# A planned attention and MLP kernel: the first theta tiles keyed four steps sooner, one threshold operation for two heads, and new cost numbers in the planner

## The chip, the core and the metric

The kernel runs on one core of one Trainium2 chip. The time is device microseconds of one launch, the median of several runs. The engines are named as in the profile: PE is the matmul engine and PEld its weight loads, DVE the vector engine, ACT the scalar engine, POOL the GpSimd engine, SP the queue that issues the transfers.

## The reference, cut to what matters

Three layers follow each other. B is 4, heads 8, sequence 576, head width 64, model width 512.

```
scores = q @ k.T / 8                         # for each batch and head
thresh = max(scores) - tau                   # row by row
scores = where(scores >= thresh, scores, -1e9)
attn   = exp(scores - max) / (sum + 1e-9);   x = attn @ v

xn = layernorm(x) * g_ln;   x = x + relu(xn @ w_ch1) @ w_ch2      # 512 -> 2048 -> 512

theta = x @ w_theta
y = w_tok_r @ (x * cos(theta)) + w_tok_i @ (x * sin(theta))
u = x + y;   out = u + relu(u @ w_ch)
```

## The kernel before

Nothing is ordered by hand. Each piece of work is an `op` with the engines that could do it and an assumed duration in nanoseconds on each, with its dependencies, with the buffer slots that it takes and frees, and with a key or an offset. `Plan.run` simulates the engines with these assumed durations: at each step it takes the engine and op that could start first, lets an op with several engines go to the one that would end it first (with a penalty for each), and emits it. PE takes the ready op with the lowest key, the other engines the one with the smallest ready time plus `OFF[kind]`. What is emitted is the fixed instruction order of each engine on the chip. So an assumed duration changes no instruction by itself. It changes which engine does an op, and in which order. The lines that the prediction speaks of are these:

- Attention goes over (batch, query tile of 128, head pair): `couple`. Each couple has two heads (`unit`), in the tail tile of 64 rows one. QK fills a PSUM tile S for each head (L720). DVE copies it negated into E and takes the minimum along the row (`top`, L784, tile `bt`). The threshold is `bt + tau` (`thresh`, L791 on ACT, L793 on POOL or DVE, tile `thr`). ACT then does the mask (L797) and the exponential (L800). P, the 16-bit high and low parts of E, is made by L222, L224 or L226 (high) and L229 (low, 512 and 64 columns apart). A transposing transfer turns P, and PE multiplies by v (L748). There are four E slots and two S slots.
- Batch 0's attention comes first. Beside it DVE, ACT and POOL split the first MLP weights into high and low parts by bit operations (`cvt`: L373 to L414, tiles `raw_w`, `a_w`, `w`).
- The MLP goes over six groups of 384 rows, first with the first half of the hidden units (`p_A`, `chA`) between attention couples, then with the second half (`p_B`, L515, and `c`, L538). The order of the second half is `(1,2), (1,0), (1,1), (0,0), (0,1), (0,2)`. A group has eight steps, and each step is one `p_B` of 12 matmuls and the `c` of 9 matmuls of the step before.
- Between them, where PE is assumed idle for more than 200 ns, `keep` puts filler matmuls (L345, tile `warm`).
- The third layer goes over batches: `transposes` (pt, L1241, tile x1T), `thetas` (th, L1288, then t and r on ACT and DVE, L1295 to L1313), `make_z` (sin, cos, products and their high and low parts z, L1363 to L1374 and L229), `mix` (y, L1451, then u, L1473 and L1478, and x1T again from u) and `chan` (o, L1508). In `mix(0)` there are four column blocks of 54 matmuls, and a block takes two of four PSUM slots, which the adds L1473 free. Transposes and thetas of batch 0 have a key in the last MLP group:

```
T0STEP = 5
KEY0 = 2e7 + 5 * nB + T0STEP + 0.3     # nB = 8 steps in a group
```

- The weights of the third layer (`th`, `tok`, `cw`) are split by `cvt` too. The third pair of `tok` tiles, `cw`, and the z tiles take slots that the last MLP group frees, one for each step.

Of the kernel before, what the change touches and what calls it, by code (L numbers as in the profile page):

```python
# [22 lines left out]
KB = 4  # L23
# [173 lines left out]
def tile_kernel(  # L197
# [48 lines left out]
    def gc(n):  # L246
        return 145.0 + 2.11 * n
# [45 lines left out]
    taup = const.tile([128, 1], F32, name="taup")  # L293
# [56 lines left out]
    def cvt(src, shape, hi, lo, name, start=(), acq=(), scales=(), kind="cvt"):  # L350
# [196 lines left out]
    class Keys:  # L547


        def __init__(self, b, hp, prev):  # L550
# [21 lines left out]
            o = op(hi, [o], A=ac(576), V=vc(576, .52), kind=kd)  # L572
# [84 lines left out]
    class Queries:  # L657


        def __init__(self, b, t, prev):  # L660
# [27 lines left out]
            o = op(hi, [o, k_tau], A=ac(512) + 93.0, V=vc(512, .52), kind=kd)  # L688
            self.ready = [op(lo, [o], (), (sraw,), V=vc(512, 1.4), G=2000, kind=kd)]

    def couple(b, t, hp):
# [36 lines left out]
        for w in us:  # L728
            pts.append(unit(w, o_qk, d, whole, pen0, kw, cp, spv, sx_ if w is us[0] else ()))
# [45 lines left out]
    def unit(st, o_qk, d, whole, pen0, kw, cp, spv, sx_):  # L775
# [40 lines left out]
        stp = Slot(rM)  # L816

        def turn_p(e):

            if "o" not in cp:  # L820
                cp["o"] = m_tile(spv, [128, 512], "pv_" + nm)
            st["tp"] = m_tile(stp, [128, 4, 128], "tp_" + nm)
            for t in range(4):
                T.transpose(st["tp"][:, t, :], st["e"][:, t * 128:(t + 1) * 128], ident)
            T.transpose(cp["o"][0:64, 256 + 128 * j:384 + 128 * j], st["e"][:, 512:576], ident)

        def take(e):
            st["pt"] = ap.tile([128, 1280], F16, tag=str(spt), name="PT_" + nm).bitcast(F32).rearrange(
                "p (t q) -> p t q", t=5)
            copy(e, st["pt"][:, 0:4, :], st["tp"])  # L830

        def take_tail(e):
            copy(e, st["pt"][0:64, 4, :], cp["o"][0:64, 256 + 128 * j:384 + 128 * j])
# [5 lines left out]
        if whole:  # L839
            o = op(turn_p, [o_mask, k_pool] + turned[-1:], (stp,) + ((spv,) + sx_ if j == 0 else ()), (es,), T=640,  # L840
                   kind="att", **kw)
            turned.append(o)
            o = op(take, [o], (spt,), (stp,), A=ac(512), V=690, kind="hi16", **kw)
            return op(take_tail, [o], A=265, V=290, kind="hi16", **kw)
        o = op(hi16, [o_mask], (s16,), A=ac(576), V=vc(576, .52), G=gc1(576), kind="hi16", pen=dict(pen0 or {}, A=HPA), **kw)
# [5 lines left out]
    def scaled(tile_):  # L851
# [25 lines left out]
        x_ops[tile_] = [op(scale, [o], V=vc(512), G=gc(512), kind="guard", pen={"G": G0} if p == 0 and t < 4 else None)]  # L877
# [7 lines left out]
    def ln_group(p, gi, base):  # L885
# [42 lines left out]
        for t in range(nt):  # L928
# [37 lines left out]
            o = first = op(norm, [o_rs, first] + last_tr, (sn,), A=808, V=vc(512, .52), kind="ln")  # L966
# [5 lines left out]
            o = op(hi, [o] + xt[:1], () if xt else (sx,), A=ac(512), V=vc(512, .52), G=gc1(512), kind="lnev")  # L972
# [153 lines left out]
    for gidx, (p, gi) in enumerate(order):  # L1126
# [4 lines left out]
        else:  # L1131
# [18 lines left out]
            o = op(hi, [o], A=ac(KB * n), V=vc(KB * n, .52), G=gc1(KB * n))  # L1150
            deps = [op(lo, [o], V=vc(KB * n), G=gc(KB * n))]
# [16 lines left out]
    def split_weight(name, src_list, start):  # L1168
# [22 lines left out]
    for i in range(3):  # L1191
# [5 lines left out]
                                 [load_of(o[-1]) for o in tok_ops])  # L1197
# [429 lines left out]
```

## Time and profile before

| | |
|---|---|
| time, median of 3 runs | 943.57 us (943.29 to 943.91) |
| the profiled execution | 943.46 us, span of its trace 941.6 us |
| mean granted TensorE clock | 0.978 of 2.4 GHz |
| busy share of the span: PE, DVE, ACT, POOL | 94%, 72%, 56%, 57% |
| stages, us from the start of the span | batch 0's attention to 132.7; attention and first MLP half to 451; last group of the first half to 486; second half to 709; third layer to the end |

The span is what the trace covers, and the execution's own time is 1.9 us longer. A row of the timeline gives start, duration, and in brackets how long the engine was idle before and who ended that. PE's durations include the waiting of a pipelined matmul and its ends are modelled, so the starts of two rows tell more than a duration.

### The profile page before, as it was taken

How to read it: one execution, taken by the hardware profiler on the slowest of the kernel's cores; microseconds unless marked ns; L12 is line 12 of the kernel's file. 1: busy time of each engine (PE TensorE's matmuls, PEld its weight loads, DVE VectorE, ACT ScalarE, POOL GpSimd, SP SyncE). 2: the span in 40 equal slices, each digit the busy share in tenths (PEclk: the TensorE clock that was granted, in tenths of full speed). 3: DMA queues.
4: the chain of work that ended last, by engine and by line, in shares of the span. 5: the costliest groups of instructions: out<-in, count | busy, mean ns of one | idle time of the engine just before them, and what ended most of it. 6: DMA issues, size and time to landing. Idle time of an engine off the chain costs nothing. (4 is left out here: it accounts for less than half of the span.)

```text
span 941.6 us, 18946 instructions
## 1 busy us (share of the span) xinstructions
PE 888.4 (94%) x7287; PEld 789.3 (84%) x7287; DVE 677.7 (72%) x1227; ACT 530.2 (56%) x968; POOL 537.7 (57%) x614
## 2 busy tenths in 40 slices
PE   9787879999999999999999999999989899999998
PEld 7665668878888888888888899989977789899998
DVE  6899989788897887783788692221489873697734
ACT  7787778888887878883556561111356330453300
POOL 5999899779887887781556771000266530263400
PEclk9898899999999999999999999999999899999999
DMA  7889796799789988792555660340021111010011
GB/s 195 171 189 184 168 199 119 138 227 176 148 180 174 184 183 145 158 165 48 190 168 168 202 190 7 100 154 1 1 77 57 28 42 39 12 63 1 14 38 51
DMA packets 224954, 111.93 MB, mean 119 GB/s; under 512 B 174048, under 2 KB 206304, under 8 KB 224864
## 3 DMA queue, kind: packets, MB, share of 16 engines
q1 hardware_dynamic: 224576, 110.72, 51.6%
q8 instruction: 57, 0.93, 0.4%
q14 instruction: 33, 0.27, 0.1%
q10 hardware_dynamic: 288, 0.00, 0.0%
HBM read 52.50 MB, written 15.73 MB: 72 GB/s over the span
## 5 line engine op out<-in xcount | busy, mean ns | idle before, releaser
L229 POOL TENSOR_TENSOR P<-E,P 128x64 f16<-128x64 f32 (+1 forms) x194 | 144.4, 759 | 14.6 <-DVE P L224 5.8
L784 DVE TENSOR_SCALAR_CACHE_REDUCE E<-S 128x576 f32<-128x576 f32 x144 | 105.4, 747 | 25.6 <-PE S L720 16.3
L797 ACT ACTIVATE E<-E,thr 128x576 f32<-128x576 f32 x144 | 108.0, 768 | 11.5 <-POOL thr L793 10.1
L515 PE MATMUL p_A<-xt,w 128*128 128x384 f32 x576 | 112.9, 343 | 1.7 <-issue 1.5
L1451 PE MATMUL y<-tok,z 128*128 128x288 f32 x768 | 109.7, 301 | 4.9 <-DVE u L1473 3.7
L515 PE MATMUL p_B<-xt,w 128*128 128x384 f32 x576 | 111.1, 341 | 1.4 <-DVE w L414 1.4
L538 PE MATMUL c<-w,h_B 128*128 128x512 f32 x432 | 108.9, 395 | 3.6 <-DVE h_B L524 2.0
L538 PE MATMUL chA<-w,h_A 128*128 128x512 f32 x432 | 111.0, 400 | 1.4 <-DVE h_A L524 1.4
L1451 PEld LDWEIGHTS y<-tok,z 128*128 128x128 f32 x768 | 106.2, 193 | 5.9 <-DVE u L1473 4.2
L515 PEld LDWEIGHTS p_B<-xt,w 128*128 128x128 f32 x576 | 103.8, 190 | 6.3 <-DVE w L414 2.3
L800 ACT ACTIVATE E<-E,ntaup 128x576 f32<-128x576 f32 x144 | 107.5, 767 | 0.9
L720 PE MATMUL S<-khi,q 64*128 64x288 f32 (+1 forms) x576 | 85.9, 328 | 21.3 <-DVE E L784 18.3
L515 PEld LDWEIGHTS p_A<-xt,w 128*128 128x128 f32 x576 | 98.2, 188 | 5.6 <-issue 4.3
L538 PEld LDWEIGHTS c<-w,h_B 128*128 128x128 f32 x432 | 80.1, 188 | 19.5 <-DVE h_B L524 3.1
L538 PEld LDWEIGHTS chA<-w,h_A 128*128 128x128 f32 x432 | 78.0, 188 | 18.2 <-issue 2.1
L748 PEld LDWEIGHTS <-PT 128*128 128x128 f16 (+1 forms) x2240 | 75.9, 101 | 17.0 <-issue 14.5
L720 PEld LDWEIGHTS S<-khi,q 64*128 64x128 f32 (+1 forms) x576 | 56.8, 192 | 37.6 <-DVE E L784 23.1
L748 PE MATMUL pv<-va,PT 128*128 128x65 f16 (+1 forms) x2240 | 84.1, 195 | 3.4 <-DVE va L224 2.3
L521 ACT ACTIVATE h_B<-p_B 128x384 fp32r<-128x384 f32 x48 | 23.6, 491 | 110.8 <-PE p_B L515 110.8
L524 DVE SCALAR_TENSOR_TENSOR h_B<-p_B,h_B 128x384 fp32r<-128x384 f32 x48 | 26.6, 553 | 72.6 <-ACT h_B L521 72.3
L229 DVE TENSOR_TENSOR P<-E,P 128x512 f16<-128x512 f32 (+1 forms) x94 | 69.6, 759 | 4.9 <-POOL P L226 3.3
L226 POOL TENSOR_SCALAR P<-E 128x576 f16<-128x576 f32 x85 | 64.7, 764 | 14.3 <-ACT E L800 13.0
(194 smaller groups left out, 1704.4 us busy)
## 6 DMA issues: line engine op xcount, KB each, us to landing
raw_w<-in_w SPq DMA_DIRECT2D x32, 512.0 KB, 4.4
raw_tok<-in_wtok SPq DMA_DIRECT2D x12, 432.0 KB, 4.3
qraw<-in_qT SPq DMA_DIRECT2D x20, 256.0 KB, 3.7
vraw<-in_v SPq DMA_DIRECT2D x16, 320.0 KB, 3.8
kraw<-in_kT SPq DMA_DIRECT2D x16, 288.0 KB, 3.2
xscr<-x SPq DMA_DIRECT2D x18, 256.0 KB, 3.1
xl<-xscr SPq DMA_DIRECT2D x18, 256.0 KB, 4.1
out<-uo SPq DMA_DIRECT2D x16, 288.0 KB, 2.1
```

Source lines behind the costliest of these rows:

```text
L226: G.tensor_scalar(out=out, in0=in_, scalar1=1.0, scalar2=0.0, op0=ALU.mult, op1=ALU.add)
L229: e.tensor_tensor(out=out, in0=a, in1=b, op=ALU.subtract)
L515: T.matmul(st["ps"][:, :n], lhsT=ch.w1(a, c), rhs=xt()[:, c, bb, :n], start=(kk == 0), stop=(kk == 11))
L521: A.activation(out=st["h"][:, 0, :n], in_=st["ps"][:, :n], func=AF.Relu)
L524: V.scalar_tensor_tensor(out=st["h"][:, 1, :n], in0=st["ps"][:, :n], scalar=0.0, in1=f(st["h"][:, 0, :n]), op0=ALU.max, op1=ALU.subtract)
L538: T.matmul(ps, lhsT=h[:, a, t * 128:(t + 1) * 128], rhs=ch.w2(bb), start=(first and (a, bb) == M2[0]), stop=(stop and (a, bb) == M2[2]))
L720: T.matmul(w["S"][:, n, 0:288], lhsT=qd.q["t"][r, a, hp], rhs=d.k[bb][r, n * 288:(n + 1) * 288], start=(k == 0), stop=(k == 2))
L748: T.matmul(out[:, j * 65:j * 65 + n], lhsT=l, rhs=r[:, j * 65:j * 65 + n], start=(k == 0), stop=(k == len(seq) - 1))
L784: V.tensor_scalar(out=st["e"].rearrange("p (a k) -> p a k", a=2), in0=st["S"][:, :, 0:288], scalar1=-1.0, scalar2=None, op0=ALU.mult, op1= ...
L797: A.activation(out=st["e"], in_=st["e"], func=AF.Prelu, bias=st["thr"], scale=-1.0, alpha=STEEP)
L800: A.activation(out=st["e"], in_=st["e"], func=AF.Exp, bias=ntaup, scale=1.0)
L1451: T.matmul(st["ps"][n][:, 0:288], lhsT=a, rhs=w[:, n * 288:(n + 1) * 288], start=(k == 0 and q == 0), stop=(k == 8 and q == 2))
```

## The change

Four things are changed. `T0STEP` is 1 and not 5. The minima of two heads stand in one tile `bt` of two columns, and one `thresh` operation adds tau to both, so that it depends on both `top` operations, and both masks depend on it. The splitting of `cw` gets a kind of its own with the offset 25000. Many assumed durations of the planner are raised: DVE's cheap copies from 157 + 0.52 n to 157 + 0.95 n, POOL's two-input operations from 145 + 2.11 n to 145 + 2.5 n, and DVE's two-input operations from 157 + 1.04 n to 157 + 1.5 n in the last phases and in `cvt`. A branch for a mode that is never used (`WHOLE` is empty) is removed. What each operation computes is the same.

```diff
-T0STEP = 5
+T0STEP = 1
+LATE = 25000.0
+GC = 2.5
+V2 = 1.5
-OFF = {..., "cvt": 6000.0}
+OFF = {..., "cvt": 6000.0, "late": LATE}
...
-        return 145.0 + 2.11 * n
+        return 145.0 + GC * n
...
+        for k in range(2):
+            V.tensor_scalar(out=taup2[:, k:k + 1], in0=taub, scalar1=0.0, scalar2=TAU_MAX, op0=ALU.max, op1=ALU.min)
...
-        o = op(s2a, [oa], G=gc1(n), V=vc(n, .52), **kw)
-        o = op(s2b, [o], V=vc(n, .52), **kw)
-        o = op(s2c, [o], (), [sa], V=vc(n), **kw)
+        o = op(s2a, [oa], G=1550.0, V=vc(n, 1.1), **kw)
+        o = op(s2b, [o], V=vc(n, .95), **kw)
+        o = op(s2c, [o], (), [sa], V=vc(n, 1.45), **kw)
...
         def thresh(e):
-            st["thr"] = ap.tile([128, 1], F32, tag="thr", bufs=8, name="thr_" + nm)
-            if e is A:
-                A.activation(out=st["thr"], in_=st["bt"], func=AF.Identity, bias=taup, scale=1.0)
+            m = len(us)
+            cp["thr"] = ap.tile([128, 2], F32, tag="thr", bufs=6, name="thr_" + nm)
+            if e is G:
+                G.tensor_tensor(out=cp["thr"][:, 0:m], in0=cp["bt"][:, 0:m], in1=taup2[:, 0:m], op=ALU.add)
+            elif e is A:
+                A.activation(out=cp["thr"][:, 0:m], in_=cp["bt"][:, 0:m], func=AF.Identity, bias=taup2[:, 0:1], scale=1.0)
...
-        o_top = op(top, [o_qk], (es,), (ss,), V=880, kind="top", **kw)
-        o = op(thresh, [o_top, k_tau], A=280, G=300, V=140, kind="thr", pen=pen0, **kw)
+        st["top"] = op(top, [o_qk], (es,), (ss,), V=830, kind="top", **kw)
+        cp.setdefault("tops", []).append(st["top"])
+        if len(cp["tops"]) < len(us):
+            return None
+        o_thr = op(thresh, cp["tops"] + [k_tau], A=290, G=320, V=160, kind="thr", pen=pen0, **kw)
+        return [u["rest"](o_thr) for u in us]
...
-        o = op(hi16, [o_mask], (s16,), A=ac(576), V=vc(576, .52), G=gc1(576), kind="hi16", pen=dict(pen0 or {}, A=HPA), **kw)
+        o = op(hi16, [o_mask], (s16,), A=ac(576), V=vc(576, .95), G=gc1(576), kind="hi16", pen=dict(pen0 or {}, A=HPA), **kw)
...
-                                 [load_of(o[-1]) for o in tok_ops])
+                                 [load_of(o[-1]) for o in tok_ops], "late")
```

Three places show what this does to the order. In the names, numbers count buffers, so p_B_2_0 is step 0 and c_2_0 the first row tile of the last group, and x12 is the count of equal rows. The lines after the change are up to eight lower.

On PE, in the last MLP group, this stands around the first transposes of batch 0 before the change:

```order
L515 MATMUL p_B_2_4_9822<-xt_0_2_9489,w_8444 128x384 x12
L1241 MATMUL pt_0_0_9841<-ident,xl_0_9408 128x128 x4
L1241 MATMUL pt_0_1_9848<-ident,xl_1_9414 128x128 x4
L1241 MATMUL pt_0_2_9858<-ident,xl_2_9419 128x128 x4
L538 MATMUL c_2_0_9755<-w_8345,h_B_2_3_9813 128x512 x3
L1241 MATMUL pt_0_3_9872<-ident,xl_3_9626 128x128 x4
L538 MATMUL c_2_1_9761<-w_8345,h_B_2_3_9813 128x512 x3
L538 MATMUL c_2_2_9766<-w_8345,h_B_2_3_9813 128x512 x3
L1241 MATMUL pt_0_4_9892<-ident,xl_4_9632 128x128 x4
L515 MATMUL p_B_2_5_9899<-xt_0_2_9489,w_8519 128x384 x12
L538 MATMUL c_2_0_9755<-w_8444,h_B_2_4_9846 128x512 x3
L1288 MATMUL th_0_9929<-th_8742,x1T_9856 128x512 x8
```

After it:

```order
L519 MATMUL p_B_2_0_9580<-xt_0_2_9355,w_7959 128x384 x12
L1233 MATMUL pt_0_0_9593<-ident,xl_0_9274 128x128 x4
L1233 MATMUL pt_0_1_9600<-ident,xl_1_9280 128x128 x4
L1233 MATMUL pt_0_2_9607<-ident,xl_2_9285 128x128 x4
L542 MATMUL c_1_0_9408<-w_8524,h_B_1_7_9571 128x512 x3
L542 MATMUL c_1_1_9415<-w_8524,h_B_1_7_9571 128x512 x3
L1280 MATMUL th_0_9623<-th_8604,x1T_9605 128x512 x6
L1233 MATMUL pt_0_3_9632<-ident,xl_3_9492 128x128 x4
L1280 MATMUL th_0_9623<-th_8604,x1T_9605 128x512 x2
L1280 MATMUL th_0_9623<-th_8618,x1T_9605 128x512 x4
L1233 MATMUL pt_0_4_9646<-ident,xl_4_9498 128x128 x4
L1280 MATMUL th_1_9653<-th_8604,x1T_9605 128x512 x8
```

The transposes stand behind step 0 and not step 4. All five theta tiles, 60 matmuls, follow at once with no MLP matmul between them, where before two stood behind step 5, two inside step 6 and one behind the last step.

On DVE, this stood behind the second theta tile of batch 0:

```order
L1313 TENSOR_SCALAR r_0_9978<-r_0_9978 128x512
L375 TENSOR_SCALAR a_cw_10025<-raw_cw_9971 128x512
L383 TENSOR_SCALAR a_cw_10025<-a_cw_10025 128x512
L1374 TENSOR_TENSOR co_0_10007<-xl_0_9408,co_0_10007 128x512
L387 TENSOR_SCALAR a_cw_10025<-a_cw_10025 128x512
L392 SCALAR_TENSOR_TENSOR raw_cw_9971<-raw_cw_9971,a_cw_10025 128x512
L375 TENSOR_SCALAR a_cw_10054<-raw_cw_10014 128x512
L383 TENSOR_SCALAR a_cw_10054<-a_cw_10054 128x512
L387 TENSOR_SCALAR a_cw_10054<-a_cw_10054 128x512
L524 SCALAR_TENSOR_TENSOR h_B_2_6_10068<-p_B_2_6_9992,h_B_2_6_10068 128x384
```

After the change, behind the third theta tile:

```order
L1290 TENSOR_SCALAR t_0_3_9740<-t_0_3_9740 128x512
L1299 SCALAR_TENSOR_TENSOR r_2_9718<-t_0_3_9740,th_3_9692 128x512
L528 SCALAR_TENSOR_TENSOR h_B_2_1_9758<-p_B_2_1_9736,h_B_2_1_9758 128x384
L1302 SCALAR_TENSOR_TENSOR r_2_9718<-t_0_3_9740,r_2_9718 128x512
L1305 TENSOR_SCALAR r_2_9718<-r_2_9718 128x512
L1366 TENSOR_TENSOR r_0_9670<-xl_1_9280,r_0_9670 128x512
L528 SCALAR_TENSOR_TENSOR h_B_2_2_9799<-p_B_2_2_9771,h_B_2_2_9799 128x384
L232 TENSOR_TENSOR z_0_9775<-co_0_9710,z_0_9775 128x512
L1290 TENSOR_SCALAR t_t_9824<-t_t_9824 128x512
L528 SCALAR_TENSOR_TENSOR h_B_2_3_9829<-p_B_2_3_9807,h_B_2_3_9829 128x384
```

Theta and z of batch 0 now stand among the `h_B` of steps 1 to 3, and the splitting of `cw`, which stood between them, comes later, among batch 1's thetas. From the first x1Tl of batch 1 to the last L1470 (L1478 before) of the four u blocks of batch 0, DVE has 65 instructions: 16 for four theta tiles, 7 of L396 (L392), 7 of L391 (L387), and 35 others.

On POOL, in batch 0, this is a stretch of attention before:

```order
L226 TENSOR_SCALAR P_0_1_2_0_880<-E_1_2_0_738 128x576
L793 TENSOR_TENSOR thr_1_3_0_888<-bt_1_3_0_876,taup 128x1
L229 TENSOR_TENSOR P_0_1_2_0_880<-E_1_2_0_738,P_0_1_2_0_880 128x64
L793 TENSOR_TENSOR thr_1_3_1_935<-bt_1_3_1_882,taup 128x1
L229 TENSOR_TENSOR P_0_1_2_0_880<-E_1_2_0_738,P_0_1_2_0_880 128x512
L383 TENSOR_SCALAR a_w_4_1_886<-a_w_4_1_886 128x512
L229 TENSOR_TENSOR P_0_1_2_1_957<-E_1_2_1_747,P_0_1_2_1_957 128x64
```

And a stretch near it after the change:

```order
L387 TENSOR_SCALAR a_w_4_1_915<-a_w_4_1_915 128x512
L798 TENSOR_TENSOR thr_2_0_1_1005<-bt_2_0_0_959,taup_93 128x2
L229 TENSOR_SCALAR P_0_1_3_0_1008<-E_1_3_0_839 128x576
L229 TENSOR_SCALAR P_0_1_3_1_1046<-E_1_3_1_886 128x576
L232 TENSOR_TENSOR P_0_1_3_0_1008<-E_1_3_0_839,P_0_1_3_0_1008 128x64
L232 TENSOR_TENSOR P_0_1_3_0_1008<-E_1_3_0_839,P_0_1_3_0_1008 128x512
L232 TENSOR_TENSOR P_0_1_3_1_1046<-E_1_3_1_886,P_0_1_3_1_1046 128x64
```

One threshold of two columns stands where two of one column did. In the whole program there are 80 thresholds and not 144 (POOL 33 and not 70, ACT 41 and not 68, DVE 6 as before). Up to the last input of the first `p_A`, POOL has 10 thresholds and not 18, 5 operations L387 (L383) and not 9, none and not 2 of v's scaling (L637), 20 subtractions P of 512 columns and not 18, and in all 120 instructions and not 140. DVE there has 5 casts of P and not 10, 14 subtractions P of 512 columns and not 17, 9 of L387 and not 5, and in all 174 and not 177. PE has 444 filler matmuls before the first `p_A` and not 415, and 96 behind it and not 72.

## Rows read from the trace of the kernel before

**Rows 1.** The page: busy time, share of the span, and instructions of each engine.

```profile
PE 888.4 (94%) x7287; PEld 789.3 (84%) x7287; DVE 677.7 (72%) x1227; ACT 530.2 (56%) x968; POOL 537.7 (57%) x614
```

**Rows 2.** Windows: start:end length, busy (instructions) of PE PEld DVE ACT POOL, granted clock, DMA.

```profile
0.00:132.70 132.70, 107.14 (x1129) 89.00 (x1129) 115.54 (x212) 100.13 (x178) 114.48 (x141) 0.90 0.84 179
132.70:451.00 318.30, 312.08 (x3448) 268.01 (x3447) 256.22 (x561) 247.56 (x460) 244.12 (x344) 1.00 0.84 161
...
656.00:690.00 34.00, 34.00 (x178) 30.54 (x177) 17.46 (x27) 13.15 (x26) 11.13 (x11) 1.00 0.05 16
690.00:763.00 73.00, 64.39 (x364) 57.11 (x364) 61.21 (x86) 37.73 (x64) 39.52 (x28) 0.95 0.16 47
763.00:811.00 48.00, 45.61 (x333) 45.05 (x331) 23.60 (x37) 9.09 (x16) 8.21 (x5) 0.96 0.11 36
```

**Rows 3.** Timeline of PE, 655 to 770: start, us, operation, count, idle before it.

```profile
675.06 1.47 PE L1241 MATMUL pt<-ident,xl 128*128 128x128 f32 x12
...
682.13 5.62 PE L1288 MATMUL th<-th,x1T 128*128 128x512 f32 x24
687.59 1.52 PE L538 MATMUL c<-w,h_B 128*128 128x512 f32 x6
...
713.21 1.04 PE L1451 MATMUL y<-tok,z 128*128 128x288 f32 x6
...
745.97 9.04 PE L1451 MATMUL y<-tok,z 128*128 128x288 f32 x47 [1.61 <-DVE u L1473]
...
762.85 2.57 PE L1508 MATMUL o<-x1T,cw 128*128 128x288 f32 x18
```

**Rows 4.** The chain that ended last, piece by piece: start, us, what.

```profile
656.37 2.10 PE p_B L515 x12
658.48 2.08 PE c L538 x9
...
764.45 1.37 DVE u L1478
...
771.10 11.88 PE o L1508 x76
```

**Rows 5.** Groups by line and form, DVE, 694 to 765: busy us, mean ns, idle before.

```profile
L1310 DVE SCALAR_TENSOR_TENSOR r<-t,r 128x512 f32<-128x512 f32 x6 | 5.8, 959 | 0.1
L392 DVE SCALAR_TENSOR_TENSOR raw_cw<-raw_cw,a_cw 128x512 uint32<-128x512 uint32 x4 | 5.3, 1316 | 0.2
L1313 DVE TENSOR_SCALAR r<-r 128x512 f32<-128x512 f32 x6 | 4.4, 731 | 0.0
...
L387 DVE TENSOR_SCALAR a_cw<-a_cw 128x512 uint32<-128x512 uint32 x4 | 3.7, 932 | 0.4 <-POOL a_cw L383 0.4
```

**Rows 6.** Groups by line and form, POOL and DVE, 0 to 132.7.

```profile
L229 POOL TENSOR_TENSOR P<-E,P 128x512 f16<-128x512 f32 x18 | 22.2, 1232 | 0.0
L229 DVE TENSOR_TENSOR P<-E,P 128x512 f16<-128x512 f32 x17 | 18.6, 1092 | 1.2 <-POOL P L226 1.2
...
L383 POOL TENSOR_SCALAR a_w<-a_w 128x512 f32<-128x512 f32 x9 | 14.5, 1616 | 0.0
...
L224 DVE CAST P<-E 128x576 f16<-128x576 f32 x10 | 8.1, 812 | 0.0
...
L793 POOL TENSOR_TENSOR thr<-bt,taup 128x1 f32<-128x1 f32 x18 | 7.0, 394 | 13.8 <-DVE vsc L616 9.6 <-DVE E L784 4.2
...
L383 DVE TENSOR_SCALAR a_w<-a_w 128x512 f32<-128x512 f32 x5 | 3.9, 786 | 0.0
L637 POOL TENSOR_SCALAR vraw<-vraw,vscale 128x640 f32<-128x640 f32 x2 | 3.4, 1692 | 0.0
```

**Rows 7.** Tile E, 20 to 132.7: the operation that fills it, and a wait of DVE.

```profile
L784 DVE TENSOR_SCALAR_CACHE_REDUCE E<-S x34: 700/746/759, 20.0 to 130.2; 128x576 f32<-128x576 f32 x34
...
  POOL P L229: 5.0, 7
```

**Rows 8.** Timeline of PE, 0 to 20: a run of filler matmuls.

```profile
10.34 2.67 PE L345 MATMUL warm<-one 128*128 128x256 bf16 x23
```

More of the change, by code (lines that the diff above doesn't have):

```diff
@@ L728, in couple @@
         for w in us:
-            pts.append(unit(w, o_qk, d, whole, pen0, kw, cp, spv, sx_ if w is us[0] else ()))
+            pts = pts + (unit(w, us, o_qk, d, whole, pen0, kw, cp, spv, sx_ if w is us[0] else ()) or [])
         def pvmm(w, out, j, cs):
@@ L773, in couple, with unit @@
             scaled(tile_)
-    def unit(st, o_qk, d, whole, pen0, kw, cp, spv, sx_):
+    def unit(st, us, o_qk, d, whole, pen0, kw, cp, spv, sx_):
         nm, j = st["nm"], st["j"]
@@ L780, in top @@
         def top(e):
-            st["bt"] = ap.tile([128, 1], F32, tag="bt", bufs=8, name="bt_" + nm)
+            if "bt" not in cp:
+                cp["bt"] = ap.tile([128, 2], F32, tag="bt", bufs=6, name="bt_" + nm)
+            st["bt"] = cp["bt"][:, j:j + 1]
             st["e"] = ap.tile([128, 576], F32, tag=str(es), name="E_" + nm)
@@ L814, in tr, with rest_of @@
             Q.dma_start_transpose(out=st["pt"], in_=st["p16"])
[L816 to L833, printed above, removed]
-        o_top = op(top, [o_qk], (es,), (ss,), V=880, kind="top", **kw)
-        o = op(thresh, [o_top, k_tau], A=280, G=300, V=140, kind="thr", pen=pen0, **kw)
+        st["rest"] = lambda o: rest_of(o, whole, pen0, kw, es, s16, spt, mask, expo, hi16, lo16, lo16t, tr)
+        st["top"] = op(top, [o_qk], (es,), (ss,), V=830, kind="top", **kw)
[4 more added lines that the diff above has]
+        return [u["rest"](o_thr) for u in us]
+    def rest_of(o, whole, pen0, kw, es, s16, spt, mask, expo, hi16, lo16, lo16t, tr):
         o = op(mask, [o], A=EXP, kind="mask", **kw)
         o_mask = op(expo, [o], A=EXP, kind="exp", **kw)
[L839 to L844, printed above, removed]
-        o = op(hi16, [o_mask], (s16,), A=ac(576), V=vc(576, .52), G=gc1(576), kind="hi16", pen=dict(pen0 or {}, A=HPA), **kw)
+        o = op(hi16, [o_mask], (s16,), A=ac(576), V=vc(576, .95), G=gc1(576), kind="hi16", pen=dict(pen0 or {}, A=HPA), **kw)
         es.uses = 2
@@ L876, in scaled @@
         o = op(recip, [o], V=190, kind="guard")
-        x_ops[tile_] = [op(scale, [o], V=vc(512), G=gc(512), kind="guard", pen={"G": G0} if p == 0 and t < 4 else None)]
+        x_ops[tile_] = [op(scale, [o], V=vc(512, V2), G=gc(512), kind="guard", pen={"G": G0} if p == 0 and t < 4 else None)]
     chunks, last_tr, hold = [], [], []
@@ L964, in spill @@
                 Q.dma_start(scr[p, gi][:, t], st["xf", t])
-            o = first = op(norm, [o_rs, first] + last_tr, (sn,), A=808, V=vc(512, .52), kind="ln")
+            o = first = op(norm, [o_rs, first] + last_tr, (sn,), A=808, V=vc(512, .95), kind="ln")
             if (p, gi) != (1, 2):
@@ L1165, in tile_kernel, with split_weight @@
     flush(pend.pop(), key + 1.5)
-    def split_weight(name, src_list, start):
+    def split_weight(name, src_list, start, kind="cvt"):
         sls = (Slot(rW), Slot(rW))
@@ L1179, in split_weight @@
             e = cvt(s_, (w,), lambda o=o, w=w: part(0, o, w), lambda o=o, w=w: part(1, o, w), f"{name}{o}",
-                    o_, sls if k == 0 else ())
+                    o_, sls if k == 0 else (), kind=kind)
             last.append(e)
```

55 lines of the change are left out of this document (27 added, 28 removed).

## The prediction

> **What bounds the kernel now.** The page's first part [rows 1] shows PE busy for 94% of the span and no other engine above 72%. So time can be gained only where PE waits or runs at the lower clock. The windows by stage [rows 2] say where that is. From 132.7 to 451 us PE is busy for 312.1 of 318.3 us, and from 656 to 690 for all 34. Three stages are different. From 0 to 132.7 PE is busy for 107.1 us at a granted clock of 0.90, and much of that is filler [rows 8]. There DVE (115.5 us) and POOL (114.5 us) work almost all the time, so these two pace batch 0's attention. From 690 to 763 PE is busy for 64.4 of 73 us at 0.95, while DVE is busy for 61.2. From 763 to 811 it is 45.6 of 48 us at 0.96. Just before, from 656 to 690, DVE is busy for 17.5 of 34 us only.
>
> The timeline of PE [rows 3] shows how the third layer starts. The transposes of batch 0 come at 675.06, the first thetas at 682.13, mix(0) at 713.21. At 745.97 PE had waited for an add of DVE (L1473), and the 47 matmuls behind it took 9.04 us. That is 0.192 us for one, where the 18 at 762.85 took 2.57, or 0.143: PE idled, and the granted clock of 1.2 GHz followed for a while. The chain of waits [rows 4] passes through DVE's u at 764.45, and PE goes on with chan(0) only at 771.10.
>
> **T0STEP, the thetas four steps sooner.** No matmul is added or removed, and PE's sum stays. Step 0 of the last group starts at 656.37 [rows 4]. A `p_B` takes 2.10 and a `c` 2.08 us. Twelve transposes take 1.47 us [rows 3], so 20 take 2.5 at most. From 682.13 to 687.59 there are 24 theta matmuls, so 60 take 13.7 us. To the end of c_2_6 PE has eight `p_B`, eight `c`, the transposes and the thetas: 16.8 + 16.6 + 2.5 + 13.7 = 49.6 us, that is 706. If nothing waits, mix(0) starts at about 709, and not at 713.21. I see no wait there: a theta tile takes PE 2.7 us. Two of DVE's four operations on it take 0.96 and 0.73 us in the later, crowded stretch [rows 5], and I estimate no more for the other two. Here DVE is half idle, and eight MLP steps follow in which it can catch up.
>
> The end of mix(0) is another matter, since DVE paces it. DVE's queue from the first x1Tl of batch 1 to the last u block has 65 instructions after the change. At the mean of the window 690 to 763 (61.21 us for 86, 0.71 us) they take 46 us. With the means of the four heavy groups [rows 5] it is 7 at 1.316, 7 at 0.932, 4 at 0.959, 4 at 0.731 and 43 at 0.71, which is 53, less 1 because three of each of the first two are 432 wide and not 512. I take 52, since these groups are of the same kind and neighbourhood. The queue starts behind the transpose at 706, so the last u ends at 759 with 1 us for waits. Before it ended at 765.8 [rows 4]. Behind it before came 5.3 us until PE went on. After the change three DVE operations follow (a product, a z and the last piece of cw), some 3.5 us as an estimate from 1.0 to 1.3 us each [rows 5]. PE then goes on with chan(0) at 762.4 and not 771.1: a gain of **8.7 us**. What limits it is DVE, not PE.
>
> Bounds: if all of PE's waiting and all of the lower clock between 690 and 763 went, it would be 8.6 + 0.05 x 73 = 12.3 us. At the lower end, the third pair of tok tiles now is split behind z of batch 0, on queues that I have counted as ready; if that takes 4 us more, 5 us stay. The late kind of cw costs nothing by itself, as long as its last piece is done with u: it stands two instructions behind the last u, and this is in the 3.5 us.
>
> **One threshold for two heads.** This takes away 64 operations. In batch 0 POOL's cost 0.394 us each [rows 6], 8 fewer are 3.2 us. The raised durations move other work off POOL too: 4 of L383 at 1.616 (6.5 us), two of L637 at 1.692 (3.4 us), and 2 more subtractions at 1.232 (2.5 us). So POOL is relieved of at least 10.6 of 114.5 us. DVE loses 5 casts at 0.812 and 3 subtractions at 1.092, and takes 4 of L383 at 0.786: 7.3 - 3.1 = 4.2 us less. The small rest nearly cancels. ACT, with 100.1 of 132.7 us busy, hides what it takes over. Against this the mask of the first head now waits for the second head's minimum, 0.746 us [rows 7]. Behind that mask are the first head's exponential, P and the E slot. DVE waited for E slots 7 times, 5.0 us together; if each were 0.75 us longer, it would cost 5.3 us. Bounds for this stage: nothing gained, to 10.6 us, POOL's own relief. I take DVE's 4.2, since DVE is the busier of the two, with the longer wait and the lighter POOL about cancelling: **4.0 us**. PE is full behind it, so the start of `p_A` carries this to the end.
>
> On the shared port, the row shows DVE's subtraction at 1.092 us and its cast of more columns at 0.812 [rows 6], so the subtraction, which reads two operands, is stretched. The Trainium skill (SBUF — State Buffer, Who interferes with whom) says that a DVE instruction with two SBUF inputs and a POOL instruction that reads SBUF exclude each other for a whole instruction. The stretched row agrees with it in kind. By it the relief of both engines would add up, and this is the second rival below.
>
> **Filler and the rest.** There are 24 more fillers behind the first `p_A`, at 2.67 / 23 = 0.116 us [rows 8]. They cost nothing where PE does idle and 2.8 us where it doesn't. I take 1.4. The other stages keep their work and nearly their order; I put 0 there, give or take 2.
>
> **Sum**, against the profiled execution's own 943.46 us, which is 0.11 below the median: 943.5 - 8.7 - 4.0 + 1.4 = **932.2 us**.
>
> **Rivals.**
> - PE limits the transition and not DVE, because with POOL less loaded DVE's operations shrink. The row against it is DVE's 61 of 73 us. 12.3 in place of 8.7: 928.6 us.
> - DVE and POOL exclude each other in batch 0, so that what either loses shortens the stage, 10.6 + 4.2 = 14.8 us: 943.5 - 8.7 - 14.8 + 1.4 = 921.4 us. Against it: POOL's and DVE's busy times overlap (230 us in 132.7).
> - Weak: the start gains nothing, since the longer wait eats the relief, the fillers cost all, and tok's third pair takes the place of the stall: 943.5 - 5 + 2.8 = 941.3 us.
> - Slower: the wait for the second minimum is exposed in couple after couple, as E slots run out. Its price is the 0.75 us of one minimum. With 8.7 gained behind it and 1.4 lost, it decides from 10 of the 64 full couples on, if batch 0 gains nothing else. With 20 exposed the time is 943.5 - 7.3 + 15 = 951.2 us. For it: the slots' 7 waits. Against it: ACT's queue is not full, so a mask mostly has room to start later.
> - Nothing changes: the thetas only swap places with the MLP, and DVE's queue ends as late as before. DVE's idle half before 690 speaks against it.
>
> **How the numbers follow.** Chances: 0.50 for the forecast (its own range 927 to 937), 0.17 for PE as the limit, 0.08 for the serial pair, 0.13 for weak, 0.08 for slower, 0.04 for no change. A measurement of this kernel can tell 0.2%, some 1.9 us, from no change. So faster has 0.88, within 0.2% has 0.04, slower 0.08. The range of 8 in 10 leaves out the slower case and part of the serial one, and holds the weak one nearly whole: 921 to 941 us.
>
> **What the profile would show.** The first `p_A` at about 129 us and not 132.7. mix(0) at about 709 less that shift. A DVE queue still above 85% from there to the last u block, with PE waiting for L1465 some 4 us and then for x1T of the last block. A clock in that stretch above 0.95. It is wrong if `p_A` starts later than now (then the joint threshold costs), if PE waits for `h_B` or an x1T inside the theta block, or if PE waits for tok in mix(0)'s first block.

## The result, and the profile after

The changed kernel takes 928.03 us (median of 4 runs, 927.37 to 929.98), the kernel before 943.43 beside it. The ratio is 0.9839, with a 95% interval of 0.9822 to 0.9856. So it is faster by 15.4 us, where 11.3 was forecast. Line numbers after are three to nine higher than before as far as the second MLP half (L784 is L790, L515 is L519), and eight lower in the third layer (L1451 is L1443).

The page's first part of the kernel after gives busy time, share and instructions of each engine, to be read beside [rows 1]:

```profile
PE 883.7 (95%) x7340; PEld 789.1 (85%) x7340; DVE 675.9 (73%) x1232; ACT 530.4 (57%) x955; POOL 510.5 (55%) x559
```

Over the whole program POOL is busy 27 us less, PE and DVE almost as long as before. The windows of the kernel after, with the columns of [rows 2], stage by stage:

```profile
0.00:132.70 132.70, 110.49 (x1259) 93.41 (x1260) 121.25 (x220) 109.05 (x190) 114.06 (x134) 0.96 0.95 196
132.70:451.00 318.30, 311.49 (x3383) 268.65 (x3382) 259.22 (x558) 240.08 (x438) 230.92 (x306) 0.99 0.83 162
640.00:690.00 50.00, 50.00 (x252) 44.20 (x252) 26.17 (x42) 21.52 (x38) 9.54 (x7) 1.00 0.08 24
690.00:763.00 73.00, 68.27 (x433) 64.16 (x432) 65.55 (x91) 38.82 (x67) 42.99 (x31) 0.95 0.26 78
763.00:811.00 48.00, 47.84 (x319) 45.05 (x319) 23.71 (x39) 12.76 (x22) 6.64 (x6) 1.00 0.06 19
```

In the first 132.7 us DVE is busy for 121.3 and ACT for 109.1, against 115.5 and 100.1: the work comes closer together. One wait of DVE shows it, that for E slots behind POOL's P, which is 5.0 us in [rows 7]. After the change (us in total, times, longest):

```profile
DVE E L790 <- POOL P L232: 1.4, 3, 1.1
```

The timeline of PE after, to be read beside [rows 3], shows the start of the third layer:

```profile
652.15 1.47 PE L1233 MATMUL pt<-ident,xl 128*128 128x128 f32 x12
...
654.85 1.53 PE L1280 MATMUL th<-th,x1T 128*128 128x512 f32 x6
...
702.42 1.05 PE L1443 MATMUL y<-tok,z 128*128 128x288 f32 x6
...
728.66 6.56 PE L1443 MATMUL y<-tok,z 128*128 128x288 f32 x48
...
743.06 2.56 PE L1500 MATMUL o<-x1T,cw 128*128 128x288 f32 x18
747.96 0.78 PE L1443 MATMUL y<-tok,z 128*128 128x288 f32 x4 [2.34 <-ACT z L225]
751.14 2.29 PE L1443 MATMUL y<-tok,z 128*128 128x288 f32 x8 [2.39 <-DVE z L232]
753.23 11.64 PE L1500 MATMUL o<-x1T,cw 128*128 128x288 f32 x78
```

From 652 to 745 PE waits for nothing. The wait for DVE's adds that [rows 3] has at 745.97 is gone. Two waits for z of the next batch, 4.7 us, stand at 745 to 751 instead. The granted clock is 1.00 from 702.4 to 747.6, and 0.95 over 690 to 763, so the lower level comes only behind the first of these waits.

To place the difference, the program is cut at three starts in PE's timeline: the second MLP half (its first `p_B`), step 0 of the last group, and the transposes of batch 2, which follow mix(1). Before, these stand at 485.9, 656.4 and 808.4; after, at 482.4, 650.0 and 791.9; and the last matmul ends at 937.8 and 921.8.

| stretch | before, us | after, us | gain | forecast |
|---|---|---|---|---|
| A: attention and first MLP half | 485.9 | 482.4 | 3.5 | 4.0 - 1.4 = 2.6 |
| B: second half up to the last group | 170.5 | 167.6 | 2.9 | 0 |
| C: last group, mix(0), chan(0), mix(1) | 152.1 | 141.9 | 10.2 | 8.7 |
| D: the rest | 129.4 | 129.9 | -0.5 | 0 |

The gains sum to 16.1 us, which is what separates the two profiled executions (943.46 and 927.37 us). In C, PE's waits sum to 10.7 us before and 4.7 after, so they are 6.0 of the 10.2; the mean granted clock of C is 0.97 and 0.98. How the rest divides was not worked out.

### The profile page after: what moved, and what is told of

Read it like the earlier page. It is cut to its first block, busy times and chain, and to the rows that moved or that the text cites. A ratio compares the mean times of both kernels' runs of the same rounds, so it can differ in the third digit from the quotient of the medians.

```text
span 925.6 us, 19016 instructions
## 1 busy us (share of the span) xinstructions
PE 883.7 (95%) x7340; PEld 789.1 (85%) x7340; DVE 675.9 (73%) x1232; ACT 530.4 (57%) x955; POOL 510.5 (55%) x559
## 4 chain that ended last, share of the span: by engine, by line
PE 71%; DVE 16%; issue 6%; POOL 4%; ACT 2%; DMA 1%; DVEq 0%; SPq 0%; POOLq 0%; ACTq 0%
PE p_A L519 11%; PE chA L542 11%; PE p_B L519 10%; PE c L542 10%; PE y L1443 7%; PE S L724 6%; PE pv L752 6%; PE o L1500 3%; PE th L1280 3%; DVE P L232 2%; DVE E L790 2%; DMA raw_w<-in_w 1%; PE warm L349 1%; DVE w L418 1%; DVE a_w L387 1%
## 5 line engine op out<-in xcount | busy, mean ns | idle before, releaser
L232 POOL TENSOR_TENSOR P<-E,P 128x64 f16<-128x64 f32 (+1 forms) x174 | 137.7, 810 | 5.1 <-ACT P L225 1.9
L790 DVE TENSOR_SCALAR_CACHE_REDUCE E<-S 128x576 f32<-128x576 f32 x144 | 104.8, 747 | 17.0 <-PE S L724 12.9
L519 PE MATMUL p_A<-xt,w 128*128 128x384 f32 x576 | 114.4, 347 | 1.4 <-POOL xt L229 1.4
L1443 PE MATMUL y<-tok,z 128*128 128x288 f32 x768 | 108.2, 298 | 4.9 <-DVE z L232 2.4
L1443 PEld LDWEIGHTS y<-tok,z 128*128 128x128 f32 x768 | 104.6, 190 | 5.8 <-DVE z L232 2.6
L806 ACT ACTIVATE E<-E,thr 128x576 f32<-128x576 f32 x144 | 105.0, 767 | 7.2 <-POOL thr L798 6.1
L519 PE MATMUL p_B<-xt,w 128*128 128x384 f32 x576 | 108.7, 337 | 0.1
L519 PEld LDWEIGHTS p_B<-xt,w 128*128 128x128 f32 x576 | 102.2, 188 | 4.5 <-DVE w L418 0.4
L519 PEld LDWEIGHTS p_A<-xt,w 128*128 128x128 f32 x576 | 100.7, 192 | 5.1 <-issue 2.5
L809 ACT ACTIVATE E<-E,ntaup 128x576 f32<-128x576 f32 x144 | 104.4, 764 | 0.0
L724 PE MATMUL S<-khi,q 64*128 64x288 f32 (+1 forms) x576 | 83.2, 321 | 20.2 <-DVE E L790 20.1
L229 POOL TENSOR_SCALAR P<-E 128x576 f16<-128x576 f32 x96 | 71.5, 750 | 38.9 <-ACT E L809 37.1
L232 DVE TENSOR_TENSOR P<-E,P 128x512 f16<-128x512 f32 (+1 forms) x114 | 89.0, 800 | 2.6 <-POOL P L229 1.9
L525 ACT ACTIVATE h_B<-p_B 128x384 fp32r<-128x384 f32 x48 | 23.6, 492 | 109.1 <-PE p_B L519 109.0
L724 PEld LDWEIGHTS S<-khi,q 64*128 64x128 f32 (+1 forms) x576 | 54.5, 186 | 35.7 <-DVE E L790 23.5
```

The source lines that it names most:

```text
L229: G.tensor_scalar(out=out, in0=in_, scalar1=1.0, scalar2=0.0, op0=ALU.mult, op1=ALU.add)
L232: e.tensor_tensor(out=out, in0=a, in1=b, op=ALU.subtract)
L519: T.matmul(st["ps"][:, :n], lhsT=ch.w1(a, c), rhs=xt()[:, c, bb, :n], start=(kk == 0), stop=(kk == 11))
L724: T.matmul(w["S"][:, n, 0:288], lhsT=qd.q["t"][r, a, hp], rhs=d.k[bb][r, n * 288:(n + 1) * 288], start=(k == 0), stop=(k == 2))
L790: V.tensor_scalar(out=st["e"].rearrange("p (a k) -> p a k", a=2), in0=st["S"][:, :, 0:288], scalar1=-1.0, scalar2=None, op0=ALU.mult, op1= ...
L806: A.activation(out=st["e"], in_=st["e"], func=AF.Prelu, bias=cp["thr"][:, j:j + 1], scale=-1.0, alpha=STEEP)
```

## The experiments

All ratios are to the kernel before, run on the same chip beside each kernel. A, B and C are the stretches of the table above, from one profiled run each. D is 129.3 to 130.0 in all of them. How far one trace can be trusted: six kernels whose order is the same in A (after, t0_back, t0_3, mix_plus, mix_minus, late_off) have A from 481.2 to 484.2, 482.5 in the mean. Nearly all of this scatter arises ahead of the first `p_A`, which comes at 127.0 to 130.4 in them; from there to the end of A they take 353.2 to 354.3. The three with the order of before in A (before, t0_alone, t0_late) have 485.9 to 486.7, and their first `p_A` at 132.7 to 132.9. C differs by 0.8 us between t0_alone and t0_late, whose orders turned out to be the same throughout. Their ratios differ by 0.0004; those of after and late_off, again one order, by 0.0003.

| kernel | ratio (95%) | A | B | C |
|---|---|---|---|---|
| before | 1 | 485.9 | 170.5 | 152.1 |
| after | 0.9839 (0.9822 to 0.9856) | 482.4 | 167.6 | 141.9 |
| t0_alone | 0.9966 (0.9951 to 0.9980) | 486.7 | 168.9 | 147.0 |
| t0_late | 0.9962 (0.9949 to 0.9974) | 486.5 | 168.9 | 147.8 |
| t0_back | 0.9999 (0.9984 to 1.0014) | 482.8 | 167.6 | 154.7 |
| t0_3 | 0.9917 (0.9902 to 0.9931) | 482.2 | 167.6 | 148.8 |
| costs_old | 0.9989 (0.9975 to 1.0003) | 493.8 | 166.0 | 147.8 |
| late_off | 0.9842 (0.9824 to 0.9861) | 481.2 | 167.6 | 142.1 |
| thr_two | 0.9874 (0.9851 to 0.9896) | 483.1 | 170.5 | 141.9 |
| nofill | 0.9884 (0.9862 to 0.9906) | 484.4 | 167.6 | 142.1 |
| mix_plus | 0.9885 (0.9869 to 0.9900) | 484.2 | 167.6 | 145.1 |
| mix_minus | 0.9836 (0.9822 to 0.9850) | 481.8 | 167.6 | 141.5 |
| b0_dve | 0.9926 (0.9913 to 0.9938) | 490.1 | 167.6 | 142.0 |
| b0_pool | 0.9908 (0.9894 to 0.9921) | 488.5 | 167.6 | 141.6 |

**t0_alone: the thetas sooner, nothing else.** The kernel before with one line changed:

```diff
-T0STEP = 5
+T0STEP = 1
```

> The kernel before with the third layer's first thetas keyed four steps sooner, and nothing else of the change. Theory of the prediction: the stretch from the last MLP group's first step to the end of mix(1) shortens by itself, by 8.7 us as forecast or by the 10.2 us that the two traces show (152.2 to 142.0), so 943.5 less 8.7 to 10.2 is 933 to 935 us, with the first p_A still at 132.7 and step 0 of the last group still at 656.4. Rival: the sooner thetas pay only in the new order, where the corrected durations put fewer and better operations in DVE's queue. Then this kernel gives at most half of that, 938.5 us or more, and PE waits inside the theta block or longer behind the last u block.

C is shorter by 5.0 us only, about half, as the rival said. mix(0) starts at 708.63 and chan(0) goes on at 763.51, almost where the prediction put them for the whole change (709 and 762.4). But inside mix(0), PE waits in its first block, as its timeline shows:

```profile
708.63 4.22 PE L1451 MATMUL y<-tok,z 128*128 128x288 f32 x30
...
720.06 0.54 PE L1451 MATMUL y<-tok,z 128*128 128x288 f32 x2 [1.62 <-ACT tok L222]
721.44 1.09 PE L1451 MATMUL y<-tok,z 128*128 128x288 f32 x3 [0.84 <-DVE tok L229]
...
761.74 0.50 PE L1508 MATMUL o<-x1T,cw 128*128 128x288 f32 x2 [3.28 <-DVE x1T L224]
763.51 2.77 PE L1508 MATMUL o<-x1T,cw 128*128 128x288 f32 x10 [1.26 <-POOL x1T L229]
```

The weight `tok` is late here. The operations on its tiles (duration min/median/max, first and last start) say by how much; t0_alone:

```profile
L366 SPq DMA_DIRECT2D raw_tok<-in_wtok x4: 327/348/370, 695.9 to 720.0; - x4
...
L222 ACT ACTIVATE tok<-raw_tok x4: 594/598/600, 715.5 to 728.2; 128x432 fp32r<-128x432 f32 x4
```

and the kernel after:

```profile
L370 SPq DMA_DIRECT2D raw_tok<-in_wtok x4: 332/352/377, 678.7 to 704.0; - x4
...
L225 ACT ACTIVATE tok<-raw_tok x4: 600/603/632, 702.1 to 718.1; 128x432 fp32r<-128x432 f32 x4
```

In t0_alone the loads of the last four pieces of `tok` begin 12.7 us ahead of mix(0)'s start, after the change 23.7 us ahead. Before the change all its conversions had started by 690, ahead of mix(0). So the sooner thetas push `tok` behind them, and something else in the change brings it forward again. The waits for `tok` are 2.5 us; the two for x1T at the end, 4.5 us, are the larger part, and why x1T is late there was not followed back.

**t0_back: all but the sooner thetas.** The kernel after with

```diff
-T0STEP = 1
+T0STEP = 5
```

> The kernel after with the first thetas keyed as before (five steps, not one). Theory: it loses the 8.7 to 10.2 us of the transition, and keeps what the joint threshold and the new durations gave, 928.0 + 8.7 to 10.2 = 937 to 938 us; the first p_A stays at 128.4. Rival: the new durations alone straighten the start of the third layer, since they also move the last pieces of cw behind the mixing work; then 930 to 933 us.

Both expectations were wrong. The rest of the change by itself is worth nothing (0.9999): A and B keep their 6 us, but C is 2.7 us longer than before. PE's waits, from its timeline:

```profile
700.68 1.33 PE L1443 MATMUL y<-tok,z 128*128 128x288 f32 x4 [5.83 <-DVE z L227]
...
737.59 2.23 PE L1443 MATMUL y<-tok,zt 128*128 128x288 f32 x6 [5.13 <-ACT zt L225]
```

Here PE starts mix(0) in the middle of the thetas, and stands at z and zt. So the thetas are worth 12.8 us in C with the rest of the change (154.7 to 141.9), and 5.0 without it.

**thr_two and nofill.** thr_two is the kernel after with a threshold operation for each head again, each with tiles of its own, planned anew; nofill is the kernel after without any of the 96 filler matmuls planned behind 125 us:

```diff
-        o_thr = op(thresh, cp["tops"] + [k_tau], ...)
-        return [u["rest"](o_thr) for u in us]
+        o_thr = op(thresh, [st["top"], k_tau], ...)
+        return [st["rest"](o_thr)]
```

```diff
-        if free and n:
+        if free and n and now < 125000.0:
```

> The kernel after with a threshold operation for each head, as before, planned with the same new durations. The prediction let the saved operations and the longer wait about cancel: 928 us give or take 1, first p_A at 128.4 give or take 1. Rival one, the wait for the second minimum costs in couple after couple: then this kernel is faster, by 3 us or more. Rival two, the saved POOL operations are the gain of the start: 8 at 0.394 us more on POOL put the first p_A 3 us later, 931 us.

> The kernel after without the filler matmuls that are planned behind 125 us; the order is otherwise the same. Prediction: the 24 additional ones cost between 0 and 2.8 us, taken at 1.4, so 926.6 us. If they stand only where PE idles: 928.0. If they hold the granted clock up: slower than 928, with a lower clock in the windows of the second and third attention stages.

thr_two is some 3 us slower than after, and its first `p_A` is 3.1 us later (131.57), the sizes of rival two. But only 0.7 us of that is left at the end of A, and the 2.9 us that it loses stand in B. The shift of `p_A` is 1.2 us beyond the scatter, that of A is within it. So rival two named the size and not the place. In B the loss is clear, since B is 167.6 in nine kernels. The joint threshold is worth 2.9 us there with either set of durations: 170.5 to 167.6 from thr_two to after, and 168.9 to 166.0 from t0_late to costs_old below. About half of it is a wait that only the kernels with a threshold for each head have, for the last pieces of the second weights (us in total, times, longest); thr_two:

```profile
PE p_B L519 <- DVE w L418: 1.4, 2, 0.9
```

In before it is 1.4 us too and in t0_alone 1.5, while PE doesn't wait for `w` there in after, t0_back and costs_old. (Before and t0_alone have one order up to the end of B. Before takes 1.6 us longer in it, with a granted clock of 0.51 from 519.5 to 523, where t0_alone has 1.00.) With the new durations no run says that the wait for the second minimum costs: in the first 132.7 us ACT waits 8.8 us for minima and thresholds after the change, 14.6 in thr_two, and 14.8 before.

nofill's ratio is 0.45% above that of after, and the intervals do not meet: the filler does not cost, it gives. A's 2.0 us are within the scatter as a whole, but from the first `p_A` to the end of A nofill takes 356.4 us, 2 to 3 more than the six. The windows say how it gives, with the columns of [rows 2]; the kernel after:

```profile
180.00:200.00 20.00, 18.89 (x211) 15.22 (x209) 14.97 (x33) 15.53 (x27) 12.84 (x18) 1.00 1.02 215
...
240.00:280.00 40.00, 38.67 (x417) 32.77 (x418) 35.49 (x76) 32.64 (x60) 35.88 (x46) 1.00 0.83 165
```

and nofill:

```profile
180.00:200.00 20.00, 16.02 (x165) 12.72 (x165) 13.96 (x32) 15.65 (x26) 12.86 (x19) 0.88 1.03 220
...
240.00:280.00 40.00, 36.18 (x386) 30.91 (x382) 33.84 (x76) 31.43 (x58) 34.80 (x47) 0.96 0.88 166
```

Where PE was left idle for 4 of 20 us, the granted clock, 1.00 of the 2.4 GHz level with filler, has a mean of 0.88, so part of that window ran at 1.2 GHz.

**mix_plus and mix_minus: does DVE set the end of mix(0)?** Both are the kernel after, with batch 1's clamp three times, or left out:

```diff
+            for _ in range(3 if b_ == 1 else 1):      # mix_plus
+            if b_ != 1:                               # mix_minus
                 V.tensor_scalar(out=r(), in0=r(), scalar1=math.pi, scalar2=-math.pi, ...)
```

> The kernel after with the clamp of batch 1's reduced angle issued three times in place of once; the repeats change nothing, and the order is otherwise the same. That is 8 more DVE operations between the transposes of batch 1 and the last u block of mix(0), at the 0.472 us that the clamp takes there: 3.8 us. If DVE's queue sets the end of mix(0), as the prediction has it, chan(0) goes on 3 to 4 us later than at 753.2, and the time is 931 to 932 us. If PE or the chain through ACT and POOL sets it, DVE has room for them: less than 1 us, 928 to 929.

> The kernel after without the clamp of batch 1's reduced angle (it leaves that bound out). Four DVE operations fewer in the same stretch, 1.9 us at 0.472. If DVE's queue sets the end of mix(0): chan(0) goes on 1.5 to 2 us sooner, 926 us. If PE is already full there up to 745 and another chain follows: 927.5 to 928.

Twelve clamps take 6.3 us in mix_plus where four take 1.9 in the kernel after, so 4.4 us are added and not 3.8. C is 3.2 us longer, and PE waits for the adds as in the kernel before. PE's timeline of mix_plus:

```profile
733.26 7.87 PE L1444 MATMUL y<-tok,z 128*128 128x288 f32 x47 [2.60 <-DVE u L1466]
```

With 1.9 us less, C is only 0.4 us shorter, and that is within the scatter. So DVE has about 1 us of room, and with it PE is full: in the kernel after, mix(0) ends when PE is through, and DVE is just quick enough.

**b0_dve and b0_pool: what paces batch 0?** The kernel after with more work for one engine:

```diff
+            if kind == "cvt1":            # b0_dve: 14 times on DVE before the first p_A, 2 behind, 256 columns
+                V.scalar_tensor_tensor(out=top[:, 0:256], in0=top[:, 0:256], ...)
+            if e is G and nm[0] == "0":   # b0_pool: 22 times on POOL, 288 columns
+                copy(e, st["p16"][:, 0:288], st["e"][:, 0:288])
```

> The kernel after, where DVE does the half of each joining operation (256 of 512 columns) a second time for the 14 weight pieces converted during batch 0's attention. That is 14 at 0.43 us, half of the 0.864 that a whole one takes: 6.0 us more on DVE, which is busy for 121 of the 132 us. If DVE paces batch 0, as the prediction has it, the first p_A comes 5 to 6 us later than at 128.4, and the time is 933 to 934. If POOL paces it: less than 2 us, 928 to 930.

> The kernel after, where POOL copies the first 288 of 576 columns of P a second time wherever it makes P in batch 0. That is 22 at 0.43 us, half of the 0.866 that a whole one takes: 9.5 us more on POOL, busy for 113 of 132 us. If POOL paces batch 0: 7 to 9 us later at the first p_A, 935 to 937. If DVE does: less than 3 us, 928 to 931. If both count because they hold each other up, this run and the one with more on DVE both show their full price.

The added operations were dearer than expected, as the groups by line show, first of b0_dve, then of b0_pool:

```profile
L399 DVE SCALAR_TENSOR_TENSOR raw_w<-raw_w,a_w 128x256 uint32<-128x256 uint32 x14 | 11.4, 817 | 0.5
```

```profile
L229 POOL TENSOR_SCALAR P<-E 128x288 f16<-128x288 f32 x22 | 12.2, 553 | 1.8
```

11.4 us more on DVE make A 7.7 us longer, or two thirds; 12.2 us more on POOL make it 6.0 longer, or half. Both fractions are rough, as A scatters by 3 us. They also depend on what is counted. The added operations on DVE take from 0.425 to 1.503 us, those on POOL from 0.431 us, and if the shortest is what one takes undisturbed, an estimate, 6.0 us of work on DVE cost 7.7 and 9.5 us on POOL cost 6.0. By that count DVE's work counts in full and POOL's for two thirds. POOL's share has a way that shows: DVE's wait for E slots behind POOL's P is 6.1 us in b0_pool, where the kernel after has 1.4. This fits DVE as the engine that sets the pace, held up by POOL through the E slots; no run isolates it.

**costs_old, late_off, t0_late, t0_3: what the thetas lacked.** late_off is the kernel after with `LATE = 6000.0`, t0_3 with `T0STEP = 3`. t0_late is t0_alone with the late kind for `cw`. costs_old is the kernel after with the old assumed durations, except those of the threshold itself:

```diff
-GC = 2.5
-V2 = 1.5
+GC = 2.11
+V2 = 1.04
...
-        o = op(s2b, [o], V=vc(n, .95), **kw)
+        o = op(s2b, [o], V=vc(n, .52), **kw)
```

> The kernel before with the first thetas keyed four steps sooner and the pieces of cw sorted as the late kind, and the old durations and two threshold operations kept. The thetas alone gave 5.0 us between step 0 of the last group and the end of mix(1), the whole change 10.2. If the late kind is what the thetas lacked, because it takes cw's conversions out of DVE's queue ahead of the last u block: that stretch takes 142 to 143 us, and the time is 933 to 934. If the new durations are what they lacked: about 147 us, 938 to 939.

> The kernel after with the assumed durations of before, and its sooner thetas, late kind and joint threshold kept. If the late kind does the rest of the transition, that stays at 142 us, and only what the durations do in batch 0 and in the conversion stage is lost: first p_A between 129 and 132, 929 to 934 us. If the durations do it: 147 us there besides, 935 to 940.

> The kernel after with the late kind given the value of the ordinary conversions (6000 in place of 25000), all else kept. The same two theories the other way round: if the late kind carries 5 us of the transition, the stretch takes 147 us and the time is 933; if the durations carry it, 142 us and 928. A third way: the pieces of cw go into DVE's idle time before 700 us, and chan(0) goes on sooner than at 753.2; then 925 to 927.

> The kernel after with the first thetas keyed two steps sooner than before, not four. If all that counts is that PE has all thetas of batch 0 behind it before the group's last steps, so that DVE catches up while the MLP runs: 928, mix(0) at the same place, since six steps of 4.2 us leave DVE 25 us. If each step sooner is worth the same, half of the 14 us between this kernel with one and with five steps is lost: 935.

The late kind does nothing at all: t0_late has the very order of t0_alone, and late_off that of the kernel after, on every engine, and their times agree. The durations do nearly all. Without them the whole change is worth 0.1% (costs_old, 0.9989). C is 147.8 us then, with the same waits for `tok` (1.61 and 0.85 us) and x1T (3.29) as t0_alone has. A is 11.4 us longer than after, and 7.3 longer than in t0_late, which differs from it by the joint threshold. So with the old durations the joint threshold costs 7.3 us in A. Part of it may be the wait for the second minimum. In the first 132.7 us ACT waits 18.0 us for minima and thresholds, against 14.8 before; costs_old:

```profile
ACT thr L800 <- DVE E L790: 11.7, 7, 3.7
ACT E L806 <- POOL thr L798: 6.3, 4, 2.8
```

and after:

```profile
ACT E L806 <- POOL thr L798: 5.5, 4, 2.4
ACT thr L800 <- DVE E L790: 3.3, 5, 1.0
```

These 3.2 us more than before do not make up 7.3. The order differs as well: DVE has 236 instructions ahead of the first `p_A`, which comes at 145.9, and 212 before and after the change. The rest stays open. Two combinations were not run: the durations alone and the joint threshold alone, both with the thetas at five steps.

In t0_3, the idea that DVE only needs some steps to catch up fell: mix(0) starts at the same place (702.05), yet C is 6.9 us longer, while PE stands 3.44 us at `tok` in mix(0) and runs at a granted clock of 0.85 from 722 to 745. Of the 12.8 us between one step and five, half is lost with three.

## Why the prediction was right, and where it was not

The forecast was 932.2 us (921 to 941), the time 928.0. The direction, the place and the rough size were right; the reasons hold in part.

- **The transition** was mis-sized: 8.7 us forecast, 10.2 measured in C. DVE's 65 instructions were put at 52 us and 1 of waiting. They took from 700.66 to 747.58, 46.9 us, close to what the plain mean of the window gives (65 at 0.71, 46.2). Taking the four heavy groups at the means of [rows 5] was the mistake: two of these means belonged to another neighbourhood. The seven of L396 fell from the 1.316 of that estimate to 0.681 (four on `raw_cw`) and 0.610 (three on `raw_tok`), L1305 from 0.731 to 0.472; L391 (0.970 and 0.832) and L1302 (0.859) stayed near theirs. DVE's groups in the kernel after, 700.6 to 753.2:

```profile
L396 DVE SCALAR_TENSOR_TENSOR raw_cw<-raw_cw,a_cw 128x512 uint32<-128x512 uint32 x4 | 2.7, 681 | 0.0
...
L396 DVE SCALAR_TENSOR_TENSOR raw_tok<-raw_tok,a_tok 128x432 uint32<-128x432 uint32 x3 | 1.8, 610 | 0.1
```

What follows the last u block was put too low, 3.5 us against 5.65. "What limits it is DVE, not PE" does not hold in the kernel after: PE runs through mix(0) without a wait, and mix_minus, with less on DVE, gains 0.4 us at most. mix_plus shows that DVE takes over as soon as it has more to do. So the rival "PE limits" had the limit right and the nearest number, 928.6, but its reason is not borne out: POOL is busy for 43.0 of 73 us there, against 41.6 in the same stretch before (700 to 773), and from mix(0)'s start to the last u block DVE's instructions take 0.68 us in the mean in both. The sign "PE waits for L1465 some 4 us" failed, PE waits for z at 745 to 751 instead.
- **What the thetas need** is the step that failed. The prediction gave the whole transition to `T0STEP` and the late kind, and took the raised durations for a relief of engines in batch 0. By t0_alone the sooner thetas give 5.0 us of C without them, which is the lower bound that the prediction named, and in part by the cause that it named, the third pair of `tok` behind z (2.5 of 7.0 us of waits for `tok` and x1T). By t0_back the durations without the thetas make C longer by 2.7. Together they give 10.2. The sum rested on the final order and not on the parts, so it held although they were put down wrongly, and in this the number was lucky. The late kind, said to cost nothing, changes no instruction.
- **Batch 0**: 4.0 us forecast; the first `p_A` came at 128.43, 4.3 sooner, and A gained 3.5 (3.9 between the means of three and six traces). The size was right, the reason was not, so this term is luck. DVE was to lose 4.2 us of work. Up to the first `p_A` it is busy for 115.5 us before and 117.0 after, so it lost none. What it lost is waiting: it stands idle for 17.2 us before and 11.5 after, and its wait for E slots behind POOL's P, which the prediction had as a cost that could grow, fell from 5.0 to 1.4. POOL was to lose 10.6 us and lost 4.7 (114.5 to 109.8). The rival in which both count in full gave 14.8 us and is far off. And order counts for more than relief: with the joint threshold and the old durations, A is 7.9 us longer than before.
- **The filler** had the wrong sign. The 24 added fillers were to cost 1.4 us; without all 96 behind 125 us the kernel is 0.45% slower. The 24 were not taken out alone.
- **Other stages** were put at 0 give or take 2. B gained 2.9, of which 1.6 are a stretch at the lower clock in the one trace before, since the same order takes 168.9 in t0_alone and t0_late. By thr_two (170.5) and costs_old (166.0) the joint threshold gives 2.9 there and the durations take back 1.6. The wait for `w` is 1.4 us of the 2.9, and the other half stays open.
- The slower rival, a joint threshold whose wait is exposed, did not come in this order: ACT waits less and not more (8.8 us against 14.8). With the old durations the joint threshold did make A 7 us longer (costs_old), though the waits seen account for 3 at most.

## What to carry to other kernels

In a planned kernel, a table of assumed durations is no bookkeeping: it decides the order, and here one key was worth 3 us, the durations with the joint threshold none, and all together 15. So time a planned change from the order that comes out of it, and test its parts in pairs, not one by one. Where a forecast number comes true, look at the wait that it was to remove: batch 0 gained what was forecast by another wait. And size a queue from the mean of a crowded stretch rather than from single groups whose neighbours will change.

## What the runs showed of the hardware

Around the two waits for z, DVE's operations on two SBUF operands have two durations, and the short one goes with a pause of POOL. DVE and POOL of the kernel after, from their timelines:

```profile
747.50 1.78 DVE L1366 TENSOR_TENSOR co<-xl,co 128x512 f32<-128x512 f32 x1
749.20 1.89 DVE L232 TENSOR_TENSOR z<-co,z 128x512 fp32r<-128x512 f32 x1
751.01 1.90 DVE L232 TENSOR_TENSOR cw<-raw_cw,cw 128x512 fp32r<-128x512 f32 x1
752.83 0.68 DVE L232 TENSOR_TENSOR z<-r,z 128x512 fp32r<-128x512 f32 x1
```

```profile
746.91 1.81 POOL L1366 TENSOR_TENSOR r<-xl,r 128x512 f32<-128x512 f32 x1
748.69 1.84 POOL L1513 TENSOR_TENSOR uo<-x1T 128x576 f32<-128x576 f32 x1
750.49 1.86 POOL L232 TENSOR_TENSOR x1T<-u,x1T 128x576 fp32r<-128x576 f32 x1
753.10 1.55 POOL L1366 TENSOR_TENSOR co<-xl,co 128x512 f32<-128x512 f32 x1 [0.74 <-ACT co L1362]
```

Each of DVE's first three operations ends some 0.5 us behind the end of a POOL operation, and takes 1.8 to 1.9 us. The fourth begins in POOL's pause of 0.74 us and takes 0.68. So for pairs like these the two engines take turns, one pair in about 1.85 us. The Trainium skill (SBUF — State Buffer, Who interferes with whom) says that such a pair excludes each other for a whole instruction, and these rows agree with it. Three such turns fill the path from the last u block to 752.9, and PE waits 2.39 us for the second. In batch 0, b0_dve and b0_pool cost two thirds and a half of the time that their added operations take, waiting included. How far the engines take turns there, and with which operations, was not tried.
